# A gated mix of a state-space layer and linear attention on one core: the written-out step list is replaced by another order of the same steps

## The chip, the cores and the metric

The kernel runs on one core of one Trainium2 chip. The metric is the device time of one execution in microseconds (us), taken without the profiler; three runs of the kernel before gave 156.17, 156.59 and 157.39 us, median 156.59. One further execution was profiled, and every number about single instructions comes from it.

The engines are named as in the profile: PE (TensorE, matrix products; PEld are its weight loads), ACT (ScalarE, functions and evictions of PSUM), DVE (VectorE), POOL (GpSimd) and SP (SyncE, which issues most of the DMAs). Each runs its own list of instructions in order and waits for the others by semaphores.

## The reference, cut to what matters

```python
x = A_x                                    # (1, 2048, 512), bf16
g = sigmoid((x * gate_w).sum(-1))          # one gate for each row
# A: a diagonal complex recurrence, 512 states
h[t] = Lam_bar * h[t-1] + x[t] @ B_bar.T   # Lam_bar = exp(dt * Lam), dt = exp(log_dt)
a = 2 * (h @ C.T).real + x * Dskip
# B: linear attention, 32 heads of 16
q, k, v = split(x @ wqkv)
pq, pk = q @ w_phi, k @ w_phi              # per head, 16 x 16
phi = concat(softmax(p), softmax(-p))      # for p = pq and p = pk: 32 features
kv, z = phi_k.T @ v, phi_k.sum(rows)
b = (phi_q @ kv) / (phi_q @ z + 1e-6) @ wo
out = g * a + (1 - g) * b
```

## The kernel before, in words

The 2048 rows are 16 tiles of 128. Row t is put in the tile of its residue t mod 8, so that the recurrence becomes eight interleaved sequences of 256 steps (two tiles each); x is held transposed (xT). The weights w_phi are folded into the query and key weights (steps W, f, w), so a tile's features come from one product.

The program is written as some 190 small generators, called steps, each of which issues a few instructions and yields. A string ORDER names the steps one by one; a loop goes through it and calls `next` on the step that each word names. So ORDER is the order in which the instructions of PE, ACT, DVE and SP are recorded, and with a manual schedule it is the order in which each of these engines runs them. A word is a step's name, then possibly `@` with the PSUM banks for its outputs, then possibly `:D` (this eviction on DVE instead of ACT) or `:A` (this output store issued from ACT's queue instead of SP's). `F:28` puts 28 dummy products on PE.

The steps that matter here (the lines are those of the kernel before):

- W0 to W3: PE transposes a block of the key weights, an eviction copies it to SBUF (line 121 on ACT, 123 on DVE). f0 to f3: the fold of w_phi into the key weights, with one eviction each. V: a PE transpose and DVE copy of the state parameters, from which U, P, P2, P3, P4 and i0 to i3 make decay rates and the tables of sines and cosines. The sines are ACT's function Sin.
- k0 to k15, v0 to v15, q0 to q15: key features, values and query features of a tile, four or eight matmuls and their evictions.
- x, n, e, s: the two softmaxes of a group of tiles. x and n (DVE, lines 519 to 535) are a tree of maxima and one of minima and the differences. e (ACT, line 140) is one Exp of 128x1024 a tile. s is a tree of sums (DVE), then Ln (ACT), Exp of its negative (ACT) and a product (DVE, line 556). The key groups 0 to 4 hold 2, 2, 4, 4 and 4 tiles. The query groups are A, 1, 2 and 3 (X1, N1, E1, S1 and so on); their s ends with an Exp called rho, a product (line 567) and DMA transposes into phT (line 579), one a tile; two tiles of group 3 are transposed on PE.
- a0 to a4: PE adds up phi_k.T @ v. Y: DVE takes it from PSUM.
- g (r, j): 8 matmuls and more for B_bar x of residue r and state block j, evicted into uv (ACT); z (j): the scan over 256 steps on DVE; h (r, j): the states of the other residues. c0 to c7: the scaled C weights, two products on ACT (line 603) and a sum on DVE; J, C, Q, R, l, NI, NR, O: input loads and DMA transposes, all issued by SP.
- y0 to y15: PE, a = h C + x Dskip of one tile, in a PSUM bank that stays open. o0 to o15: PE forms numerator and denominator (pn, line 753), ACT takes Ln and Exp for the division and the gate, DVE multiplies, and the result is transposed, by DMA (line 775) or for o12 to o15 on PE. t0 to t15: PE adds o @ wo to the open bank (line 782), an eviction scales by the gate (line 786 on ACT, 788 on DVE), a DMA stores the tile (line 790).
- L: closes the pool of the tables' temporaries, opens the one of the scan, and calls `pin_act_set` (line 131). ACT evaluates functions from a loaded set. `pin_act_set` records a load of the set `natural_log_exp_and_others`, which holds both Exp and Ln. Where a function is not in the set that was loaded last, the build puts a load ahead of it by itself.

```python
    def pin_act_set():
        pre = nc.scalar.preload_act_table_set(ACT_SET)
...
    def st_L():
        pin_act_set()
        tab_g.__exit__(None, None, None)
        enter("sw", name="ssm", bufs=2)
        yield
```

`pin_act_set` is called twice: once ahead of the list (line 171), and once in L. The Sin of the tables needs a set of its own, so that before the first e there is no longer a set with Exp loaded.

Of the kernel before, what the change touches and what calls it, by code (L numbers as in the profile page):

```python
# [23 lines left out]
ORDER = """
NI l8 l10 F:28 W1@0 W0@1 W0 B W2@2 W2 NR W1:D W3@3 f1@4 f1 W3:D V@5 V U f0@6 U P P P2 U P2 P2 P2 P2 f0 f2@0 P4 P4 P4
V2@1 V2 f2 l9 P3 i3 f3@3 f3 F:4 k1@2 k0@4 P P2 P3 l12 i1 i0 k0 gw i0 i3 U k1 i3 i3:D i3 i0 i1 i1 k2@5 k2 k3@6 k3 v0@03
k4@1 i0:D x0 i1:D l11 x0 i1 n0 F:4 x0 k4 n0 R0 i2 n0 i0 x0 n0 k5@4 i2 i2 x0 i2:D n0 x1 x1 k5 n1 i2 v3@25 v0 x1 k7@6 k7
k6@7 R1 L e0 n1 n1 x1 n1 l13 k6:D v4@14 x1 l14 v1@03 v1 k10@6 n1 x2 v4 n2 n2 n2 x2 e0 s0 x2 v3 v7@70 v7 l15 k8@3 v2@14
v6@25 s0 s0 k9@7 k12@0 x2 Q1 e1 s0 v2 v6 s0 k11@1 s0 e1 M k11 k8 D k10 k9 R3 k12 g40@4 g40 s0 s1 g00@2 g00 n2 a0@51 a0
v5@36 v5 s1 R5 x2 v8@70 R2 v8 C5 s1 s1 s1 s1 g60@4 n2 x3 s1 g60 g30@2 x3 n3 x3 n3 g10@3 C3 g20@6 e2 e2 e2 e2 x3 a1 a1  # L30
n3 Q2 k15@7 g10 g10 k15 x3 n3 g20 k14@0 k14 s2 n3 R4 s2 k13@4 g01@3 Q0 k13 n4 s2 g30 g01 x4 s2 x4 Q3 n4 x4 g50@7 g70@6
g30 g50 n4 x4 e3 e3 g41@0 g50 n4 R7 s2 g21@4 s2 g70 s2 C7 e3 g31@3 e3 s3 g62@2 C4 g70 g70 z0 g11@7 a2 z0 s3 g41 z0 a2
a2 s3 C6 g21 g62 C2 C1 g11 g11 C0 J0 w0@6 w1@0 J2 J2 a2 g22@4 J0 w2@2 x4 s3 J1 g31 w1 w0 w3@7 g22 g31 z0 z0 z0 s3 w2
s3 n4 z0 z0 w3 g61@0 g51@6 g51 g61 g02@4 g51 e4 g02 g71@3 g71 g71 g71 q3@2 s3 g12@7 g12 e4 q2@0 z0 g12 z1 q3 q1@6 q1
q0@4 q2 z1 z0 h50@3 z1 z1 g42@7 q0 z1 z1 v10@26 h50 xA z1 h10@0 e4 e4 z1 g42 nA s4 g32@4 v10 g32 a3 g52@3 g32 h60@7 c2
xA s4 c4 O g52 xA c4 R6 z1 z1 v9@26 s4 h10 g52 nA g72@4 g72 c4 h60 v9 a3 J3 g03@3 v11@26 c2 c2 s4 g72 g72 c0 c0 nA
g63@0 z2 z2 v12@74 a3 nA v11 a3 xA g03 z2 z2 z2 z2 xA nA s4 J3 g63 g23@2 c5 s4 v12 g23 h51@6 g13@3 g13 g13 z2 z2 c0 z2
z2 eA g43@0 g43 eA v14@74 v14 J1 h51 s4 g33@2 g33 h52@3 g33 h12@0 g53@6 eA g53 g53 h12 h11@7 h11 h52 eA sA g73@4 g73
g73 g73 v13@26 v13 q10@0 z3 c6 z3 c5 sA z3 z3 v15@73 z3 a4 a4 a4 v15 z3 q10 q5@4 a4 Y z3 h31@0 q5 sA h30@4 z3 q9@2 h31
q13@6 h31 q9 h33@0 h61@7 Y q13 h30 sA sA c5 h62@3 z3 z3 h30 h61 sA Y Y h22@5 q4@2 h62 q4 h33 q15@6 q11@7 h22 h20@4 h20  # L40
h32@2 h32 sA sA c1 q11 h13@1 h13 h32 q14@3 h40@5 h33 c3 h53@7 h42@4 sA h42 h53 c1 c1 sA h21@2 c3 h21 q6@0 q6 q15 c6
q7@1 h63@4 h63 q8@7 h03@0 c3 q7 c6 h40 sA c7 h41@6 h41 y6@2 c7 h03 h03 h43@4 h43 y2@1 h02@5 c7 sA h23@6 h23 h01@0
h00@4 END q8 G X1 y6 y6 q14 y2 N1 X1 h00 h00 N1 y2 h02 h02 X1 N1 G h01 o0@6 y0@7 o0 o0@3 h01 o2@4 o2 X1 o2@5 o2 o2 N1
y5@6 o0 y3@0 X1 N1 y5 X2 o0 o1@4 E1 o2 y0 o2 o0 E1 E1 E1 X2 y1@5 y1 y3 y3 o1 G N2 X2 N2 X2 o0 N2 X2 o3@3 o3 o3@4 S1 o3
o3 G S1 N2 S1 t2 o3 S1 o3 t2 t2:A q12@3 q12 N2 S1 S1 o1@4 o1 o1 o1 o1 S1 S1 E2 S1 y0 y4@1 y9@3 y8@4 y8 y8 X3 E2 E2 S1
S1 S1 N3 X3 E2 t3 X3 X3 X3 S2 N3 t0 t0 t0:A S2 t3 S2 y1 t1 t1 y5 y9 y9 o4@7 o4 o4@0 o4 y4 o4 o4 o4 o5@5 o5 o5@7 o5 o5
y13@0 S2 S2 o6@5 o6 o6@7 o6 o6 y13 N3 y7@5 y7 N3 y7 y13 o5 S2 S2 N3 E3 o5 o6 o6 S2 S2 E3 E3 o7@7 o7:D y4 t4 t4:D t5
o7@7 S2 S2 E3 S3 t5 S2 S3 S3 o7 o7 o7 t6 y11@1 y11 o7 t6 o8@6 o8 o8@7 o8 o8 S3 S3 o8 y12@2 o9@6 o9 o9@7 o8 y11 y12 y12
y10@6 o9 o9 o9 o11@7 o11 o9 S3 S3 y10 y10 o11@7 t7 o11 o11 t7 t8 S3 S3 o11 o11 S3 t8 S3@7 S3:D S3@5 S3 t9 t9 t1:A
o10@4 y15@7 o10:D o10@5 o10:D t8 o10 o10 o10 y15 o12@4 o12:D o12@3 t4 o14@5 o12 o12 o12 t5 o14 t11 o14@4 o14:D o14 o14  # L50
t11 y14@3 t9:A o13@5 o13 o12@4 o12:D y14 o13@1 o13 o13 o15@4 o15:D o15@5 o15 o15 t12 t3:A t10 o13 o13@1 o15 t6:A t11
o14@4 o13:D t7 t10 t10 y15 t12 t12 o15@5 o15 y14 o14:D t13 t14 t14 t14 t13 t13 t15 t15 t15:A
"""
# [811 lines left out]
```

## Time and profile before

| | |
|---|---|
| time, median of three runs | 156.59 us (156.17 to 157.39) |
| profiled execution: span from the first to the last instruction (its time as a whole is not listed) | 153.7 us |
| PE busy | 145.5 us (95%) |
| DVE busy | 131.0 us (85%) |
| ACT busy | 136.7 us (89%) |
| mean granted TensorE clock | 0.995 |
| bytes by DMA | 17.03 MB |

The profile's page lists the busy time of each engine and the chain of work that ended last. Further views group instructions by line, give the busy time of each engine in chosen windows of the span, and list instructions in order of time: start, length, engine, line, operation, the tiles written and read, and, in square brackets, how long the engine sat idle before it and what ended that. A row with x4 merges four instructions that follow each other. A matmul's row is longer than the distance to the next one, since PE pipelines them, and ACT's rows overlap a little for the same reason, so the distance between starts is the better measure of what an instruction costs.

### The profile page before, as it was taken

Reading aid. Unit: us, or ns where it says so; the run is one execution under the profiler, and the core shown is the slowest. Engines: PE = TensorE matmul, PEld = TensorE weight load, DVE = VectorE, ACT = ScalarE, POOL = GpSimd, SP = SyncE. Lnnn points to the kernel's source line nnn. Section 1 sums busy time; section 2 is a strip of 40 time slices with the busy share of each in tenths; the row PEclk is TensorE's granted clock in tenths of the full one; section 3 lists DMA queues with packets and bytes.
Section 4 is the critical chain, followed back from the end, with each engine's and each line's share of the span. In section 5 each row is a group of like instructions: output and inputs, shape, how many; then the busy total and the mean of one; then the engine's idle time right before and its main releaser. Section 6 shows DMA issues by size and latency. Waiting matters only on the chain.

```text
span 153.7 us, 3412 instructions
## 1 busy us (share of the span) xinstructions
PE 145.5 (95%) x1238; PEld 99.7 (65%) x1254; DVE 131.0 (85%) x302; ACT 136.7 (89%) x322; POOL 12.9 (8%) x43
## 2 busy tenths in 40 slices
...
GB/s 117 162 220 121 213 171 102 102 86 92 101 102 100 80 146 205 237 133 0 2 4 2 0 0 134 125 18 68 33 82 118 215 80 194 141 118 172 211 123 102
DMA packets 48737, 17.03 MB, mean 111 GB/s; under 512 B 42064, under 2 KB 48720, under 8 KB 48720
## 3 DMA queue, kind: packets, MB, share of 16 engines
...
q8 instruction: 10, 0.16, 0.5%
q0 software_dynamic: 160, 0.01, 0.2%
q14 instruction: 7, 0.06, 0.1%
...
## 4 chain that ended last, share of the span: by engine, by line
ACT 48%; PE 31%; DMA 8%; DVE 6%; issue 3%; POOL 2%; ACTq 0%; POOLq 0%
PE py L734 12%; ACT EEk L140 12%; ACT uv L121 9%; PE py L782 6%; ACT vx L121 5%; PE pq L478 5%; ACT Xq L121 5%; ACT phT L603 4%; PE ph L685 3%; ACT va L121 3%; DMA phT<-EEq 3%; DMA oT<-on 3%; PE pn L753 2%; DMA vec_n<-in_A_log_dt_dram 2%; ACT EEq L140 2%
## 5 line engine op out<-in xcount | busy, mean ns | idle before, releaser
L614 PE MATMUL pgq<-xT,BT 128*128 128x256 bf16 x256 | 31.5, 272 | 0.0
L614 PEld LDWEIGHTS <-BT 128*128 128x128 bf16 x256 | 24.7, 98 | 3.5
L140 ACT ACTIVATE EEk<-EEk 128x1024 bf16<-128x1024 bf16 x20 | 21.3, 1099 | 0.0
L478 PEld LDWEIGHTS <-xT 128*128 128x128 bf16 x128 | 12.2, 97 | 11.0 <-issue 0.2
L121 ACT CAST uv<-pgq 128x512 bf16<-128x512 f32 x28 | 16.7, 638 | 0.0
L492 PE MATMUL pv<-Wv,xT 128*128 128x256 bf16 (+1 forms) x128 | 16.5, 273 | 0.1
L478 PE MATMUL pq<-Wq,xT 128*128 128x512 bf16 x60 | 15.2, 379 | 0.2
L782 PE MATMUL py<-Wo,oT 128*128 128x512 bf16 x59 | 14.7, 379 | 0.6 <-DMA oT<-on 0.3
L478 PE MATMUL pk<-Wk,xT 128*128 128x512 bf16 x60 | 14.9, 379 | 0.2
L492 PEld LDWEIGHTS <-xT 128*128 128x128 bf16 x128 | 12.5, 98 | 3.1 <-issue 0.2
L786 ACT ACTIVATE ot<-py,G 128x512 bf16<-128x512 f32 x15 | 9.8, 684 | 2.9 <-PE py L782 2.4
L140 ACT ACTIVATE EEq<-EEq 128x1024 bf16<-128x1024 bf16 x12 | 11.8, 1084 | 0.3 <-DVE EEq L535 0.3
L603 ACT ACTIVATE phT<-X,dgB 128x512 bf16<-128x512 bf16 x16 | 11.1, 751 | 0.0
L140 ACT ACTIVATE ld<-pn 128x16 f32<-128x16 f32 x32 | 6.4, 204 | 5.2 <-PE pn L753 5.0
L121 ACT CAST vx<-pv 128x256 bf16<-128x256 f32 x32 | 10.7, 435 | 0.0
L121 ACT CAST nu<-pn 128x256 bf16<-128x256 f32 x26 | 10.0, 400 | 0.0
L556 DVE TENSOR_TENSOR EEk<-EEk,rck 128x4096 bf16<-128x4096 bf16 (+1 forms) x5 | 9.3, 1860 | 0.1
L121 ACT CAST Xq<-pq 128x512 bf16<-128x512 f32 x16 | 9.0, 604 | 0.4 <-PE pn L753 0.4
L782 PEld LDWEIGHTS <-oT 128*128 128x128 bf16 x64 | 5.7, 98 | 5.7 <-DMA oT<-on 0.5
L753 PEld LDWEIGHTS <-phT 128*128 128x128 bf16 x128 | 6.4, 97 | 4.6 <-DMA phT<-EEq 1.3
L761 DVE TENSOR_TENSOR on<-nu,rd 128x512 bf16<-128x512 bf16 x16 | 6.6, 422 | 2.6 <-ACT rd L140 2.1
L519 DVE TENSOR_TENSOR smk<-smk 128x512 bf16<-128x512 bf16 (+4 forms) x18 | 8.1, 449 | 0.1
...
## 6 DMA issues: line engine op xcount, KB each, us to landing
...
out_dram<-ot SPq DMA_DIRECT2D x9, 128.0 KB, 2.2
out_dram<-ot ACTq DMA_DIRECT2D x7, 128.0 KB, 2.0
...
```

What stands on the lines that cost most here:

```text
L121: nc.scalar.copy(out=out_ap, in_=in_ap)
L140: ins = nc.scalar.activation(**kw)
L478: MM(out=pt[:], lhsT=xT[:, kt, ti * P:(ti + 1) * P], rhs=W[:, kt, :], start=(kt == 0), stop=(kt == KT - 1))
L492: MM(out=pv[c][:], lhsT=xT[:, kt, ti * P:(ti + 1) * P], rhs=Wvg[:, kt, c * hd:(c + 1) * hd + c], start=(kt == 0), stop=(kt == KT - 1))
L519: VT(out=dst, in0=cur[:, :, :, 0:n, :], in1=cur[:, :, :, n:2 * n, :], op=op)
L556: VT(out=E5, in0=E5, in1=rc.to_broadcast([P, L, 2 * NB, Dh, 4]), op=ALU.mult)
L603: nc.scalar.mul(out=t_, in_=x_, mul=c_)
L614: MM(out=pg[:, h, :], lhsT=BT[:, kt, 2 * j + h, :], rhs=xT[:, kt, r * NC:(r + 1) * NC], start=(h == 0 and kt == 0), stop=(r % 2 == 0 and k ...
L734: MM(out=py[:], lhsT=hs(r, t, slice(a * P, (a + 1) * P)), rhs=C2B[t], start=(t == 0), stop=False)
L753: MM(out=pn[:, 4 * m:4 * m + 4, :].rearrange("p h e -> p (h e)"), lhsT=ph[:, 4 * hf + m, :], rhs=KVm[:, 4 * hf + m, :], start=(m == 0), st ...
L782: MM(out=py[:], lhsT=oT[:, g, :], rhs=Wo[:, g, :], start=False, stop=(g == HG - 1))
L786: nc.scalar.mul(out=ot[:], in_=py[:], mul=G[:, ti:ti + 1])
```

## The change

The string ORDER is replaced by another one, with the same 862 words apart from banks and sides; no generator changes. The new string has one line more, so that each line number after it is one higher. The core of the diff:

```diff
-NI l8 l10 F:28 W1@0 W0@1 W0 B W2@2 W2 NR W1:D W3@3 f1@4 f1 W3:D V@5 V U f0@6 U P P P2 U P2 P2 P2 P2 f0 f2@0 P4 P4 P4
-V2@1 V2 f2 l9 P3 i3 f3@3 f3 F:4 k1@2 k0@4 P P2 P3 l12 i1 i0 k0 gw i0 i3 U k1 i3 i3:D i3 i0 i1 i1 k2@5 k2 k3@6 k3 v0@03
-k4@1 i0:D x0 i1:D l11 x0 i1 n0 F:4 x0 k4 n0 R0 i2 n0 i0 x0 n0 k5@4 i2 i2 x0 i2:D n0 x1 x1 k5 n1 i2 v3@25 v0 x1 k7@6 k7
-k6@7 R1 L e0 n1 n1 x1 n1 l13 k6:D v4@14 x1 l14 v1@03 v1 k10@6 n1 x2 v4 n2 n2 n2 x2 e0 s0 x2 v3 v7@70 v7 l15 k8@3 v2@14
-v6@25 s0 s0 k9@7 k12@0 x2 Q1 e1 s0 v2 v6 s0 k11@1 s0 e1 M k11 k8 D k10 k9 R3 k12 g40@4 g40 s0 s1 g00@2 g00 n2 a0@51 a0
-v5@36 v5 s1 R5 x2 v8@70 R2 v8 C5 s1 s1 s1 s1 g60@4 n2 x3 s1 g60 g30@2 x3 n3 x3 n3 g10@3 C3 g20@6 e2 e2 e2 e2 x3 a1 a1
-n3 Q2 k15@7 g10 g10 k15 x3 n3 g20 k14@0 k14 s2 n3 R4 s2 k13@4 g01@3 Q0 k13 n4 s2 g30 g01 x4 s2 x4 Q3 n4 x4 g50@7 g70@6
-g30 g50 n4 x4 e3 e3 g41@0 g50 n4 R7 s2 g21@4 s2 g70 s2 C7 e3 g31@3 e3 s3 g62@2 C4 g70 g70 z0 g11@7 a2 z0 s3 g41 z0 a2
...
-y5@6 o0 y3@0 X1 N1 y5 X2 o0 o1@4 E1 o2 y0 o2 o0 E1 E1 E1 X2 y1@5 y1 y3 y3 o1 G N2 X2 N2 X2 o0 N2 X2 o3@3 o3 o3@4 S1 o3
-o3 G S1 N2 S1 t2 o3 S1 o3 t2 t2:A q12@3 q12 N2 S1 S1 o1@4 o1 o1 o1 o1 S1 S1 E2 S1 y0 y4@1 y9@3 y8@4 y8 y8 X3 E2 E2 S1
-S1 S1 N3 X3 E2 t3 X3 X3 X3 S2 N3 t0 t0 t0:A S2 t3 S2 y1 t1 t1 y5 y9 y9 o4@7 o4 o4@0 o4 y4 o4 o4 o4 o5@5 o5 o5@7 o5 o5
-y13@0 S2 S2 o6@5 o6 o6@7 o6 o6 y13 N3 y7@5 y7 N3 y7 y13 o5 S2 S2 N3 E3 o5 o6 o6 S2 S2 E3 E3 o7@7 o7:D y4 t4 t4:D t5
-o7@7 S2 S2 E3 S3 t5 S2 S3 S3 o7 o7 o7 t6 y11@1 y11 o7 t6 o8@6 o8 o8@7 o8 o8 S3 S3 o8 y12@2 o9@6 o9 o9@7 o8 y11 y12 y12
-y10@6 o9 o9 o9 o11@7 o11 o9 S3 S3 y10 y10 o11@7 t7 o11 o11 t7 t8 S3 S3 o11 o11 S3 t8 S3@7 S3:D S3@5 S3 t9 t9 t1:A
-o10@4 y15@7 o10:D o10@5 o10:D t8 o10 o10 o10 y15 o12@4 o12:D o12@3 t4 o14@5 o12 o12 o12 t5 o14 t11 o14@4 o14:D o14 o14
-t11 y14@3 t9:A o13@5 o13 o12@4 o12:D y14 o13@1 o13 o13 o15@4 o15:D o15@5 o15 o15 t12 t3:A t10 o13 o13@1 o15 t6:A t11
-o14@4 o13:D t7 t10 t10 y15 t12 t12 o15@5 o15 y14 o14:D t13 t14 t14 t14 t13 t13 t15 t15 t15:A
+F:28 W0@3 W0 W1@4 B W2@1 W3@6 l10 l8 NI W1:D f1@2 NR W2:D W3:D f1:D l9 f2@4 V@6 V l11 f2 U l12 P P f0@5 f0 l14 R0 R1
+P2 l15 P2 P2 P2 f3@0 U P2 V2@4 V2 P4 f3 P F:4 P2 k1@6 k1 k0@3 k0 gw P4 P4 P3 P3 l13 i3 i1 Q1 i0 k3@1 U i0 i3 i1 k2@0
+i3 i0 v0@46 i3:D i3 i1 i1:D R4 R2 n0 k2 v0 k4@5 C3 k3 i0:D R3 n0 x0 F:4 i1 k5@3 n0 i2 R5 x0 i0 C2 v1@10 n0 k4 x0 i2 x0
+i2 k5 v4@47 i2:D k6@2 k7@3 i2 x0 x1 n0 e0 n1 x1 n1 n1 k7 x1 v1 C4 n1 k6:D x1 Q3 k10@6 U e0 x1 n1 n2 v3@52 v4 x2 n2 s0
+s0 v3 v7@31 v7 x2 k8@0 k8 s0 x2 s0 v2@47 v2 v6@35 C1 M D k9@2 s0 k11@0 k12@1 e1 s0 s0 e1 s1 g40@4 v6 k12 k11 k9 g40 C5
+k10 g00@3 a0@51 g00 a0 v5@07 v5 n2 s1 n2 v8@42 s1 x2 g60@6 Q0 s1 s1 v8 x2 k14@7 x3 s1 g20@0 g60 n2 s1 e2 e2 e2 e2
+k13@3 a1 a1 Q2 g10@2 g10 g20 g10 k15@4 R6 k15 n3 g30@6 k13 x3 n3 x3 n3 x3 g01@0 n3 x3 k14 s2 n3 s2 g30 g01 x4 g21@4
+g30 e3 g50@0 g31@7 s2 e3 x4 s2 s2 n4 n4 x4 L g50 g50 s2 n4 g62@2 g70@6 x4 n4 e3 e3 g70 g70 g70 g41@0 s2 g41 g21 s3
+g11@3 g11 g11 C7 a2 a2 a2 a2 z0 z0 s3 z0 z0 C6 z0 w0@6 s3 w1@0 O w1 z0 s3 g62 z0 g22@4 g22 w2@3 w2 z0 g31 x4 g31 g61@2
+g61 s3 w0 g51@4 g51 s3 g51 g02@7 g02 w3@6 g71@2 g71 n4 s3 w3 q0@4 q1@7 e4 q3@6 g71 g71 e4 q0 z0 z1 z1 q3 q2@2 q2 z0 z1
+q1 C0 J0 J2 J1 J2 g12@0 g12 h10@3 J1 g12 h50@2 z1 z1 z1 e4 h10 nA g42@4 g72@7 g32@0 g42 xA h50 z1 z1 c2 xA e4 g32
...
+h03 q8 y6 h00@0 y2 h02@6 q14 h01@3 h23 h43 END X1 N1 h00 h00 y2 y0@7 G X1 h02 o0@5 o0 o0@4 N1 X1 o0 N1 h02 y0 o2@0 o2
+o2@4 X1 o2 h01 h01 y1@5 y5@6 N1 o2 o0 o3@4 X1 N1 X2 o2 o0 X2 G o1@3 X2 y3@0 y1 y1 N2 X2 o2 N2 y3 X2 E1 E1 E1 E1 S1 N2
+o1 o3 y0 y5 t2 o3@3 o3 S1 o3 t2 o3 o0 t0 y5 t0 o1@3 o1 S1 q12@4 q12 y3 N2 y4@1 S1 S1 y8@3 y8 y8 N2 S1 y6 o1 o1 o3 o1
+S1 t3 S1 S1 S1 y4 y9@4 S1 S1 t1 E2 E2 E2 X3 X3 y4 t3 E2 t1 o4@7 o4 o4@0 N3 X3 o4 N3 o4 y9 y9 X3 o5@7 o5 o5@5 o5 o5 N3
+y13@0 o6@7 X3 S2 S2 o6 o4 S2 N3 o6@5 o6 S2 S2 o5 y13 N3 y13 o7@7 o6 y7@5 y7 S2 o7 S2 o4 t4 E3 E3 E3 o5 o6 o6 S2 t5
+t4:D o7@7 S2 S2 E3 o7:D y11@1 t6 y11 t5 t6 y7 o7 S2 o8@7 o8 S3 S3 o7 S3 o8@6 y12@2 o8 o8 o9@7 o8 o9 o9@6 y12 y12 o9 S3
+y10@6 y10 y10 o9 S2 o7 o8 o11@7 o9 y11 t7 S3 S3 t5:A o9 S3 o11 S3 S3 t7:D o11@7 t1:A o11 o11 o11 t8 t8:D S3 S3@7 S3
+S3@5 S3:D t9 t8:A o11 t9:D o10@3 o10:D o10@5 o10 y15@7 o14@5 t4:A t7 o12@4 o10 o12:D o12@3 o12 o14 y15 y15 o14@4 o13@5
+o12 o10 o13:D o13@3 o14:D t11 o14 o15@5 t0 o13:D y14@4 o12 o15:D o12@3 o13 o14 o15@5 o15 o10 t3 y14 y14 o13 o15 o15
+t10 o12 t9 t11 t11:A o14@3 o15@5 o15 o13@1 o13 o14:D t12 t10:D t12:D t14 t15 t10 t14:D t13 t2 t13:D t15 t12:A t14:A
+t13:A t6 t15
```

What moves, by the order of the built instructions:

- L goes from the fourth line of the list, ahead of e0, to the eighth, behind e0, e1, e2, the first two words of e3, and the Ln of s0, s1 and s2. The built list of ACT holds 3 loads of function sets before, 9 after.
- The evictions of W2 and f1 go from ACT to DVE. In the last quarter of the list the scalings of t7, t8, t9, t10, t12, t13 and t14 go from ACT to DVE, and some small evictions of o7, o10, o12, o13 and S3 change sides both ways. SP issues eight of the 16 output stores, ACT eight; before, nine and seven. The stores of t0, t2 and t6 come much later in the list.
- Up to the last word of E1, ACT's list holds the same instructions in both, apart from the six loads and the evictions of W2 and f1. PE's products ahead of o4 are nearly the same ones in both.
- The order of g, h, q, v, c and y among each other changes nearly everywhere, and with it the order of the loads and DMA transposes on SP.

18 lines of the change are left out of this document (7 added, 11 removed).

## The prediction

> **What bounds the kernel now.** I read the page's busy times first, then the view by windows, then the timeline of ACT, then the chain that ended last.
>
> ```profile
> span 153.7 us, 3412 instructions
> ...
> PE 145.5 (95%) x1238; PEld 99.7 (65%) x1254; DVE 131.0 (85%) x302; ACT 136.7 (89%) x322; POOL 12.9 (8%) x43
> ...
> ACT 48%; PE 31%; DMA 8%; DVE 6%; issue 3%; POOL 2%; ACTq 0%; POOLq 0%
> ```
>
> Three engines are nearly full and the chain runs through two of them, so no one engine "is" the bound over the whole span. The windows (length, then busy microseconds of PE, PEld, DVE, ACT, POOL) say where each of them is full:
>
> ```profile
> 0.00:10.00 10.00, 7.81 (x73) 6.42 (x75) 5.66 (x37) 5.64 (x10) 4.92 (x17) 1.00 0.62 162
> ...
> 18.00:46.00 28.00, 27.87 (x256) 21.74 (x256) 27.69 (x54) 27.86 (x63) 0.66 (x3) 1.00 0.64 114
> 46.00:100.00 54.00, 53.42 (x479) 40.31 (x480) 53.38 (x113) 53.65 (x116) 0.00 (x0) 1.00 0.41 84
> 100.00:107.30 7.30, 7.24 (x52) 3.73 (x52) 7.30 (x18) 7.30 (x20) 0.00 (x0) 1.00 0.19 42
> 107.30:118.10 10.80, 10.69 (x77) 5.75 (x77) 10.56 (x20) 9.38 (x22) 0.00 (x0) 1.00 0.55 74
> 118.10:149.60 31.50, 30.54 (x268) 17.03 (x270) 18.48 (x39) 23.82 (x75) 0.00 (x0) 1.00 0.66 156
> ```
>
> From 18 to 107.3 us ACT is idle for 0.14 + 0.35 + 0.00 = 0.5 us in 89. After that it has room: 1.4 us up to 118.1 and 7.7 us up to 149.6. PE is full to the end: from 118.1 to 149.6 it is idle for 0.96 us only. So anything put on ACT before 107.3 us has no hole to fall into, and anything that delays PE at 118 us moves the end.
>
> Busy time can flatter an engine whose rows overlap, so I look at the pitch of ACT's rows. Each row is start, length, engine, line:
>
> ```profile
> 8.86 0.21 ACT L140 ACTIVATE ssm_par<-ssm_par 128x4 f32<-128x4 f32 x1
> 9.09 1.28 ACT L146 ACT_TABLE_LOAD   x1
> ...
> 16.93 0.64 ACT L121 CAST Xq<-pk 128x512 bf16<-128x512 f32 x1
> 17.59 1.28 ACT L132 ACT_TABLE_LOAD   x1
> 18.89 1.06 ACT L140 ACTIVATE EEk<-EEk 128x1024 bf16<-128x1024 bf16 x1
> ...
> 32.51 3.90 ACT L140 ACTIVATE EEk<-EEk 128x1024 bf16<-128x1024 bf16 x4
> 36.31 0.57 ACT L121 CAST uv<-pgq 128x512 bf16<-128x512 f32 x1
> 36.78 0.59 ACT L121 CAST Xq<-pk 128x512 bf16<-128x512 f32 x1
> ```
>
> Four exponentials start 0.95 us apart (32.51 to 36.31), a 512-wide eviction is followed after 0.47 us (36.31 to 36.78): ACT issues without a gap. And a table load is not free: the eviction of 16.93 would be followed at 17.40, but the load waits for its end (17.57), starts at 17.59, takes 1.28, and the exponential starts at 18.89. The load costs 18.89 - 17.40 = 1.49 us of ACT there; its bare length is 1.28.
>
> **The change part by part.** The order listing of the two built programs shows the same 1254 matmuls and the same arithmetic. Four things differ.
>
> *1. Table loads.* In the old list the step L (the load of the set that has both Exp and Ln) stands before the first exponential, e0. In the new list it stands far behind, after group 2's Ln; e0, e1, e2 and the sums s0, s1, s2 run before it. Then the build puts a load wherever the next function isn't in the loaded set. The built ACT lists have 3 loads before and 9 after: one before e0, then before the Ln and again before the next Exp of s0/e1, the same two for s1, one for the Ln of s2, and L itself. That is six more, all between e0 (18.89 us in the old run) and the last exponentials of e3, in the chain
>
> ```profile
> 42.94 1.89 ACT EEk L140 x2
> ```
>
> where ACT has 0.14 us to spare. Bare price 6 x 1.28 = 7.7; with the drain of the row above, 6 x 1.49 = 8.9. The Trainium skill (ScalarE: Activation LUTs, "What ACT_TABLE_LOAD costs") gives 1283 ns for a load plus about 1380 ns of drain, 2.66 us for a switch. The trace agrees on the load and not on the drain: the exponential starts 0.02 us after the load. By the page the term would be 6 x 2.66 = 16 us (an estimate).
>
> *2. Two evictions leave ACT early.* W2 and f1 go to DVE.
>
> ```profile
> 5.39 1.07 ACT L121 COPY Xq<-ptw 128x512 bf16<-128x512 bf16 x2 [2.22 <-PE ptw L277]
> ...
> 4.12 0.69 DVE L346 TENSOR_TENSOR BD<-Wc,mask 128x512 bf16<-128x512 bf16 x1 [1.42 <-DMA Wc<-in_B_w_phi_dram]
> 4.97 0.42 DVE L123 COPY Xq<-ptw 128x512 bf16<-128x512 bf16 x1 [0.16 <-PE ptw L277]
> 5.97 0.42 DVE L123 COPY Xq<-ptw 128x512 bf16<-128x512 bf16 x1 [0.57 <-PE ptw L277]
> 6.98 0.17 DVE L315 CAST vec<-pvt 128x12 f32<-128x12 bf16 x1 [0.59 <-PE pvt L313]
> ```
>
> They take 1.0 off ACT (the row of two copies is 1.07 long with its tail, so some 0.5 each, and 0.47 is the pitch of a 512-wide cast above). On DVE they cost 0.42 for the copy and about 0.6 for the cast (nearest row: a 512-wide f32 vector operation, below, 0.68), 1.0 in all, ahead of the step V. DVE idles 0.16 + 0.57 + 0.59 = 1.3 us there, which hides them; uncovered, they'd delay the table chain by 1.0.
>
> Everything else that ACT does up to the last exponential of E1 (the first query group) is the same set of instructions in both lists, only permuted. So ACT's stock of work at that point grows by 7.7 to 8.9 less 1.0: **6.7 to 7.9 us**. I take 7.2, nearer the bare load, because its waits on others (at most the 0.5 us above) vanish when it is the late one.
>
> *3. What E1 releases.* The timelines of ACT, DVE, SP and PE around it, then the median landing from the page's DMA issues, then one row of the chain:
>
> ```profile
> 103.50 4.00 ACT L140 ACTIVATE EEq<-EEq 128x1024 bf16<-128x1024 bf16 x4
> ...
> 107.54 1.23 DVE L519 TENSOR_TENSOR smq<-EEq 128x2048 bf16<-128x2048 bf16 x1
> ...
> 112.41 1.22 DVE L567 TENSOR_TENSOR EEq<-EEq,rhoq 128x2048 bf16<-128x2048 bf16 x1
> ...
> 113.80 6.68 SPq L579 DMA_TRANSPOSE phT<-EEq  x4
> ...
> 118.18 0.42 PE L753 MATMUL pn<-KVm,phT 128*128 128x68 bf16 x8
> ...
> 119.83 0.43 PE L753 MATMUL pn<-KVm,phT 128*128 128x68 bf16 x8 [0.36 <-DMA phT<-EEq]
> ...
> phT<-EEq SPq DMA_TRANSPOSE x10, 2.8
> ...
> 115.15 4.63 DMA phT<-EEq
> ```
>
> E1 ends at 107.5, the sum tree starts at 107.54, the product with rho ends at 113.63, the transposes are issued from 113.80. The first lands about 2.8 us later, 116.6, and o4's matmuls (118.18) come 1.6 us after it. The second, issued at 115.15, lands at 119.78, and o5 starts at 119.83: no slack. So a delay of 7.2 at E1 reaches PE as 5.6 (o4) to 7.2 (o5). The second transpose shared the DMA engines with the store of t0, which the new list moves away from there, so I count 1.0 of slack: 6.2. In both lists the same PE work lies behind o4, the 30.5 busy us of the last window, and its 0.96 us of holes are all that can be given back; I take half, 0.5.
>
> *4. The end, and the DMA queues.* Seven scalings of the output tile (line 786), those of t7 to t10 and t12 to t14, go from ACT to DVE; of the steps o and S3 a few small evictions change sides both ways.
>
> ```profile
> L786 ACT ACTIVATE ot<-py,G 128x512 bf16<-128x512 f32 x15 | 9.8, 684 | 2.9 <-PE py L782 2.4 <-ACT ot L786 0.4
> ...
> L689 DVE TENSOR_TENSOR HM<-ph,uv 128x512 bf16<-128x512 f32 x8 | 5.3, 682 | 0.0
> ...
> 110.09 0.36 ACTq L790 DMA_DIRECT2D out_dram<-ot  x1
> ...
> 148.80 1.84 ACT L786 ACTIVATE ot<-py,G 128x512 bf16<-128x512 f32 x3 [1.10 <-PE py L782]
> ...
> out_dram<-ot SPq DMA_DIRECT2D x9, 128.0 KB, 2.2
> ```
>
> The last three scalings stand in line on ACT (1.84 us). Split over two engines the last one ends about one place, 0.6 us, sooner (a DVE form of that width isn't in the trace; the nearest row is 0.68, the same as ACT's 0.684). Against it, two early stores (t2, t6) are held back to the end of SP's list: two more issues, at about 0.35 us each, and 256 KB more in the last 3 us. Below: nothing, since t15's store waits for its scaling anyway; above 0.7. I take 0.2. Net of the end: -0.4. The input loads, transposes and J copies are permuted on SP early; with ACT late they have more time, so nothing, and 1.35 us (the first two issues above are 1.35 apart) for one that were out of place. One store more on ACT's queue lies in ACT's idle 7.7 us.
>
> Sum: 7.2 - 1.0 - 0.5 - 0.4 = +5.3 us. The profile gives its execution's span alone: 153.7 becomes 159.0. The median of the runs, 156.6, is 2.9 above it, and that stays. **156.6 + 5.3 = 161.9 us.**
>
> **The rivals.**
> *The loads are hidden.* PE, not ACT, sets the pace, and each load falls into a wait of ACT. For it: the chain runs through PE lines for 31%, and PE is as full as ACT. Against: ACT's 0.5 us of idle in 89. Time: the ends of the list alone, about 156.6 - 0.4 = 156.2.
> *Faster.* PE at its own pace, with its holes closed by the new order: 0.13 + 0.58 + 0.06 + 0.11 + 0.96 = 1.8 us from 18 us on, and 0.4 at the end. It needs ACT to reach the end of E1 no later than 107.5 + 1.0; then 154.4. PE's 2.2 idle us of the first 10 stay: ACT's first eviction (5.39) still waits for the transposes of the same weights.
> *It adds up.* All six at 1.49, the 1.0 us on DVE uncovered, no slack at o5, nothing given back: 8.9 - 1.0 + 1.0 = +8.9, 165.5. For it: all engines run their lists in order, so a late ACT can make PE and DVE late for each other too. Against: whoever waits for a late ACT gains time on everything else that it would have waited for.
> *The full drain.* If after each load ACT stood still for about its own length again, the shift would be near 6 x 2.6 = 15.6, less 1.0, 1.0, 0.5 and 0.4: 169.3. Row 18.89 speaks against it. The Trainium skill's section on table loads named above is what would have it so.
> That the loads aren't there is no case: the built list has them, and the three that the old built list has are the three in its trace.
>
> **How the numbers follow.** Forecast 0.72 (159 to 164.5), adding up 0.13, full drain 0.03, hidden 0.07, faster 0.05. One per cent, 1.6 us, is about what a measurement of this kernel tells from no change (its runs lie within 156.17 to 157.39). Slower 0.72 + 0.13 + 0.03 = 0.88, within 1% 0.07, faster 0.05. The range takes in the forecast and the adding-up case with its price at either end: low 6.7 - 1.6 - 1.0 - 0.6 = +3.5 would be 160, and I go to 157.8 for half-hidden loads; high 166.5.
>
> **What would show it.** Right: nine table loads in the groups of the profile after, those on line 141 with 1.28 us each between 19 and 50 us; ACT full and PE with holes of 4 to 6 us in that stretch; the last E1 exponential ending near 114.7 instead of 107.5; o4 on PE near 124; from there to the last matmul 31 us again. Wrong: ACT waiting just before its loads (hidden), E1 ending before 109 (faster), or E1 late and the last matmul not (then the tail had slack that I don't see).

## The result and the profile after

The new list takes **165.16 us** (median of four runs, 165.10 to 165.41) against 156.50 us (156.17 to 157.39) for the old one: a ratio of **1.056, interval 1.052 to 1.059**, so 8.7 us more. The prediction was 161.9 us, with 157.8 to 166.5 as its range. The time lies in the range, but 3.3 us above the forecast and outside the forecast's own band of 159 to 164.5; it is within 0.4 us of the rival "it adds up" (165.5). Of the experiments below, one execution of new_l_early_oldsp (160.47 us) and one of new_to_E1_old_tail (159.89) were over 1.5% longer than the fastest of their kernel and are left out of the medians.

The page of the kernel after, its span, busy times, clock in 40 slices and the shares of the chain that ended last:

```profile
span 163.4 us, 3418 instructions
...
PE 148.4 (91%) x1238; PEld 100.1 (61%) x1254; DVE 136.3 (83%) x310; ACT 140.8 (86%) x320; POOL 14.7 (9%) x43
...
PEclk9999999997899999999999999999999999999998
...
PE 57%; ACT 26%; DMA 8%; DVE 6%; issue 1%
```

The span grew by 9.7 us. Busy time grew by 4.1 on ACT, 2.9 on PE and 5.3 on DVE, so each of the three idles more than before: a wait was added, not just work. The profiled execution of before was a short one: the timed runs, before and after, last 2.0 us longer than their spans (165.41 and 163.4), so its time was some 155.7 us (an estimate: 153.7 + 2.0), 0.8 below the median, where the prediction took 2.9 from a single profile. That is why 9.7 us of span are 8.7 us of time. All shifts against rows of before, below, are shifts against that short execution; where in it the 0.8 us were saved no run shows.

The view by windows of the kernel after (length, then busy us of PE, PEld, DVE, ACT, POOL; then clock, DMA share and GB/s):

```profile
18.00:46.00 28.00, 23.66 (x183) 16.28 (x184) 23.11 (x47) 27.28 (x58) 3.88 (x8) 0.94 0.70 128
46.00:100.00 54.00, 52.07 (x492) 41.09 (x493) 49.76 (x106) 53.62 (x112) 0.00 (x0) 1.00 0.35 65
...
128.00:159.50 31.50, 28.81 (x247) 16.29 (x252) 20.79 (x41) 20.62 (x65) 0.00 (x0) 1.00 0.69 152
```

From 18 to 46 us ACT is nearly as full as it was (0.72 us idle against 0.14), and PE and DVE, which had been full too, idle 4.3 and 4.9 us. That is the place of the loss. In the last 31.5 us before the last product PE idles 2.7 us, where it idled 0.96 before: a second, smaller loss.

The timeline of ACT in the first stretch (start, length, engine, line, then what ended the idle time):

```profile
16.94 1.28 ACT L141 ACT_TABLE_LOAD   x1
18.24 1.06 ACT L141 ACTIVATE EEk<-EEk 128x1024 bf16<-128x1024 bf16 x1
19.20 0.57 ACT L122 CAST Xq<-pk 128x512 bf16<-128x512 f32 x1
...
24.29 1.28 ACT L141 ACT_TABLE_LOAD   x1
25.58 0.31 ACT L141 ACTIVATE lgk<-smk 128x128 f32<-128x128 f32 x1
25.91 1.28 ACT L141 ACT_TABLE_LOAD   x1
27.20 1.06 ACT L141 ACTIVATE EEk<-EEk 128x1024 bf16<-128x1024 bf16 x1
...
43.00 1.56 ACT L122 CAST Xq<-pk 128x512 bf16<-128x512 f32 x3 [0.41 <-PE pk L479]
44.74 1.07 ACT L122 CAST uv<-pgq 128x512 bf16<-128x512 f32 x2 [0.18 <-PE pgq L615]
...
47.74 1.28 ACT L141 ACT_TABLE_LOAD   x1
49.03 0.42 ACT L141 ACTIVATE lgk<-smk 128x256 f32<-128x256 f32 x1
49.47 1.28 ACT L133 ACT_TABLE_LOAD   x1
50.76 0.58 ACT L122 CAST uv<-pgq 128x512 bf16<-128x512 f32 x1
...
51.56 1.99 ACT L141 ACTIVATE EEk<-EEk 128x1024 bf16<-128x1024 bf16 x2
```

The same two exponentials of e3 in the kernel before:

```profile
42.85 1.99 ACT L140 ACTIVATE EEk<-EEk 128x1024 bf16<-128x1024 bf16 x2
```

The loads stand where the prediction put them: one round each Ln, with the next row 0.01 to 0.02 us behind each. The last exponentials of e3 start 51.56 - 42.85 = 8.71 us later. That sum can be taken apart: e0 starts 0.65 us earlier (18.24 against 18.89), six loads are 7.70, two waits for PE are 0.41 + 0.18 = 0.59, and ACT has one key eviction more between e0 and e3 (nine casts from pk into Xq, as the one at 19.20, against eight; before, it stood ahead of e0), which is 0.47 us at the pitch of such casts. 8.71 + 0.65 - 7.70 - 0.59 - 0.47 = 0.60 us is left for six loads, 0.10 each, beside the 1.28.

The groups of ACT's loads (times, busy us, mean ns):

```profile
L141 ACT ACT_TABLE_LOAD x6 | 7.7, 1283 | 0.1
...
L133 ACT ACT_TABLE_LOAD x2 | 2.6, 1283 | 1.9 <-issue 1.9
...
L147 ACT ACT_TABLE_LOAD x1 | 1.3, 1283 | 0.0
```

Nine, as forecast. From e3 on the shift hardly changes. The timelines of ACT, SP and PE round E1 in the kernel after:

```profile
112.29 3.94 ACT L141 ACTIVATE EEq<-EEq 128x1024 bf16<-128x1024 bf16 x4
...
122.75 6.53 SPq L580 DMA_TRANSPOSE phT<-EEq  x4
...
126.48 0.42 PE L754 MATMUL pn<-KVm,phT 128*128 128x68 bf16 x8
...
128.73 0.43 PE L754 MATMUL pn<-KVm,phT 128*128 128x68 bf16 x8 [0.75 <-DMA phT<-EEq]
```

Against the rows of before: E1 +8.79, the transposes of S1 +8.95, o4 +8.30, o5 +8.90. The end, from PE's timeline, the chain and DVE's timeline:

```profile
139.23 5.07 DMA oT<-on
...
144.35 1.04 PE L783 MATMUL py<-Wo,oT 128*128 128x512 bf16 x4 [1.69 <-DMA oT<-on]
...
155.97 3.62 PE L783 MATMUL py<-Wo,oT 128*128 128x512 bf16 x15
...
159.63 0.75 DVE L789 TENSOR_SCALAR ot<-py,G 128x512 bf16<-128x512 f32 x1 [0.97 <-PE py L783]
```

The last product ends at 159.59 instead of 149.62: +9.97, that is o4's 8.30 and 1.7 us of new holes. One hole of 1.69 us stands ahead of t7, which waits for the DMA transposes of o7.

### The profile page after: what moved, and what is told of

Read it like the earlier page. It is cut to its first block, busy times and chain, and to the rows that moved or that the text cites. A ratio compares the mean times of both kernels' runs of the same rounds, so it can differ in the third digit from the quotient of the medians.

```text
span 163.4 us, 3418 instructions
## 1 busy us (share of the span) xinstructions
PE 148.4 (91%) x1238; PEld 100.1 (61%) x1254; DVE 136.3 (83%) x310; ACT 140.8 (86%) x320; POOL 14.7 (9%) x43
## 4 chain that ended last, share of the span: by engine, by line
PE 57%; ACT 26%; DMA 8%; DVE 6%; issue 1%
PE pgq L615 12%; PE py L735 12%; PE pq L479 8%; PE py L783 7%; ACT L141 5%; ACT EEk L141 5%; PE ph L686 4%; PE pv L493 4%; DMA oT<-on 3%; ACT vx L122 3%; ACT Xq L122 3%; DMA phT<-EEq 3%; ACT uv L122 2%; PE pn L754 2%; DMA C2r<-in_B_wqkv_dram 2%; PE kvacc L595 2%
## 5 line engine op out<-in xcount | busy, mean ns | idle before, releaser
L615 PE MATMUL pgq<-xT,BT 128*128 128x256 bf16 x256 | 32.7, 277 | 2.2 <-ACT vx L122 1.9
L479 PEld LDWEIGHTS <-xT 128*128 128x128 bf16 x128 | 12.3, 99 | 11.6 <-issue 0.5
L604 ACT ACTIVATE phT<-X,dgB 128x512 bf16<-128x512 bf16 x16 | 11.9, 765 | 0.0
L789 DVE TENSOR_SCALAR ot<-py,G 128x512 bf16<-128x512 f32 x8 | 6.0, 749 | 4.9 <-PE py L783 4.8
L122 ACT CAST nu<-pn 128x256 bf16<-128x256 f32 x25 | 9.2, 387 | 0.0
L122 ACT CAST Xq<-pk 128x512 bf16<-128x512 f32 x15 | 8.5, 608 | 0.4 <-PE pk L479 0.4
```

The lines of the kernel that those rows point to most:

```text
L122: nc.scalar.copy(out=out_ap, in_=in_ap)
L479: MM(out=pt[:], lhsT=xT[:, kt, ti * P:(ti + 1) * P], rhs=W[:, kt, :], start=(kt == 0), stop=(kt == KT - 1))
L604: nc.scalar.mul(out=t_, in_=x_, mul=c_)
L615: MM(out=pg[:, h, :], lhsT=BT[:, kt, 2 * j + h, :], rhs=xT[:, kt, r * NC:(r + 1) * NC], start=(h == 0 and kt == 0), stop=(r % 2 == 0 and k ...
```

## The experiments

The theory was that six loads on a full ACT make the loss, whatever else the new order does. The rivals were that the new order itself makes it (through PE, SP's transfers or the end), and that a single one of the other edits does. All comparisons are with the kernel before on the same chip. Each of these kernels computes the whole output; where the words Z add loads, they load the set that is loaded already, so they change nothing but time.

### The new order without the loads: new_l_early

```diff
-i2 k5 v4@47 i2:D k6@2 k7@3 i2 x0 x1 n0 e0 n1 x1 n1 n1 k7 x1 v1 C4 n1 k6:D x1 Q3 k10@6 U e0 x1 n1 n2 v3@52 v4 x2 n2 s0
+i2 k5 v4@47 i2:D k6@2 k7@3 i2 x0 x1 n0 L e0 n1 x1 n1 n1 k7 x1 v1 C4 n1 k6:D x1 Q3 k10@6 U e0 x1 n1 n2 v3@52 v4 x2 n2 s0
...
-g30 e3 g50@0 g31@7 s2 e3 x4 s2 s2 n4 n4 x4 L g50 g50 s2 n4 g62@2 g70@6 x4 n4 e3 e3 g70 g70 g70 g41@0 s2 g41 g21 s3
+g30 e3 g50@0 g31@7 s2 e3 x4 s2 s2 n4 n4 x4 g50 g50 s2 n4 g62@2 g70@6 x4 n4 e3 e3 g70 g70 g70 g41@0 s2 g41 g21 s3
```

> The new list with the word L moved back to just ahead of e0: 3 table loads instead of 9, all else as in the new list. Theory A (the six loads on a full ACT are the whole loss, and the permutation is worth about nothing): 165.2 - 8.8 = 156.4 us, between 155.5 and 157.0, and the last exponential of E1 starts near 106.3 as in the old list. Theory B (the new order itself is worse, the loads cost only what they can't hide): 160 to 163 us, E1 near 110.

Measured: 160.09 against 156.85 us, ratio 1.021 (1.018 to 1.024): +3.2 us. With three loads the new list is 5 us faster than with nine, but the permutation has a price of its own. That is the time of theory B; theory A, by which the permutation is worth nothing, fails here, and so does the prediction, which had it as a gain (-1.0 for the two evictions, -0.4 for the end). Its waits (who waits for whom: us in total, times, longest) show where a part of it is:

```profile
PEld L435 <- DMA HM<-in_B_wqkv_dram: 1.4, 2, 0.8
ACT phT L604 <- DMA X<-HM: 1.4, 1, 1.4
```

The first is for a transposed weight block (a step Q), the second for a copy J; both were moved on SP's list. In the kernel after, with its nine loads, neither wait is there.

### The loads without the new order: old_l_late

```diff
-k6@7 R1 L e0 n1 n1 x1 n1 l13 k6:D v4@14 x1 l14 v1@03 v1 k10@6 n1 x2 v4 n2 n2 n2 x2 e0 s0 x2 v3 v7@70 v7 l15 k8@3 v2@14
+k6@7 R1 e0 n1 n1 x1 n1 l13 k6:D v4@14 x1 l14 v1@03 v1 k10@6 n1 x2 v4 n2 n2 n2 x2 e0 s0 x2 v3 v7@70 v7 l15 k8@3 v2@14
...
-g30 g50 n4 x4 e3 e3 g41@0 g50 n4 R7 s2 g21@4 s2 g70 s2 C7 e3 g31@3 e3 s3 g62@2 C4 g70 g70 z0 g11@7 a2 z0 s3 g41 z0 a2
+g30 g50 n4 x4 e3 e3 g41@0 g50 n4 R7 s2 L g21@4 s2 g70 s2 C7 e3 g31@3 e3 s3 g62@2 C4 g70 g70 z0 g11@7 a2 z0 s3 g41 z0 a2
```

> The old list with L moved behind the Ln of s2, where the new list has it: 9 loads instead of 3, nothing else moved. Theory A: six loads of 1.28 plus the drain of about 0.19 each, 8.9 us on ACT; no eviction moved and at most 1 us of slack behind E1, so 156.5 + 8 to 9 = 164.5 to 165.5 us. Theory B: 158 to 160 us, since in the old order they would be partly hidden.

Measured: 165.20 against 156.85 us, ratio 1.052 (1.050 to 1.055): +8.35 us, as theory A had it. One word moved in the old list costs as much as the whole change. Its ACT timeline, the windows, and PE's first products of o4:

```profile
19.10 1.06 ACT L140 ACTIVATE EEk<-EEk 128x1024 bf16<-128x1024 bf16 x1
...
52.02 1.99 ACT L140 ACTIVATE EEk<-EEk 128x1024 bf16<-128x1024 bf16 x2
...
18.00:46.00 28.00, 23.28 (x184) 16.30 (x184) 22.71 (x45) 27.35 (x56) 0.79 (x4) 0.94 0.61 114
46.00:100.00 54.00, 51.43 (x493) 41.22 (x494) 49.56 (x105) 53.56 (x112) 0.00 (x0) 1.00 0.36 67
...
127.35 0.42 PE L753 MATMUL pn<-KVm,phT 128*128 128x68 bf16 x8
```

From e0 to e3 the list takes 52.02 - 19.10 = 32.92 us where it took 23.96: +8.96, or 1.49 a load. Of that, 0.52 us are two new waits of ACT for PE (0.23 and 0.29, between 42 and 46 us); without them it is 8.44, or 1.41 a load. At e3 the shift is 9.17, and at o4 it is 9.17 still (127.35 against 118.18). In the rows nothing is given back in 75 us. The windows have the pattern of the kernel after: PE 4.7 us idle in the first stretch.

### Is it ACT's time, or the place of L? old_z6_mid

L stays where it was; a new word Z loads the same set again, six times between 24 and 47 us.

```diff
-v6@25 s0 s0 k9@7 k12@0 x2 Q1 e1 s0 v2 v6 s0 k11@1 s0 e1 M k11 k8 D k10 k9 R3 k12 g40@4 g40 s0 s1 g00@2 g00 n2 a0@51 a0
+v6@25 s0 s0 k9@7 k12@0 x2 Q1 e1 s0 v2 Z:1 v6 s0 k11@1 s0 e1 M k11 k8 D k10 k9 Z:1 R3 k12 g40@4 g40 s0 s1 g00@2 g00 n2 a0@51 a0
...
+        if tok == "Z":
+            for _ in range(int(eng)):
+                act_st["pre"] = nc.scalar.preload_act_table_set(ACT_SET)
+            continue
```

> The old list with L in its place and six superfluous loads of the same set put behind the steps v2, k9, v5, v8, g1 0 and k13, which run between 24 and 37 us. Theory A: as old_l_late, 164.5 to 165.5 us, since only ACT's time counts. Theory C (what hurts is that L, which also changes the pools, comes late): near 156.5 us.

Measured: 164.62 against 156.85 us, ratio 1.048 (1.046 to 1.051): +7.8 us, 1.30 a load. So the loss needs neither L's late place nor loads beside the Ln: six loads at other places of the full stretch make 7.8 of the 8.35 us.

### Half the loads: old_l_mid

```diff
-v5@36 v5 s1 R5 x2 v8@70 R2 v8 C5 s1 s1 s1 s1 g60@4 n2 x3 s1 g60 g30@2 x3 n3 x3 n3 g10@3 C3 g20@6 e2 e2 e2 e2 x3 a1 a1
+v5@36 v5 s1 R5 x2 v8@70 R2 v8 C5 s1 s1 L s1 s1 g60@4 n2 x3 s1 g60 g30@2 x3 n3 x3 n3 g10@3 C3 g20@6 e2 e2 e2 e2 x3 a1 a1
```

(and L taken out ahead of e0, as above; three loads more instead of six)

> The old list with L just ahead of the Ln of s1: 6 loads instead of 3. If each load costs its length and the drain, 1.49 us, and nothing of it is hidden: 156.85 + 4.5 = 161.3 us, half of what six cost. If the first ones are hidden and only a pile of them hurts: 157 to 159 us.

Measured: 160.23 against 156.73 us, ratio 1.023 (1.020 to 1.025): +3.5 us, 1.17 a load, somewhat less than the load's own 1.28 and 1.1 us below the expected 161.3. The price is about in proportion to the count, 1.2 to 1.4 a load by the times. The first and the last exponential of e0 to e3, from ACT's timeline:

```profile
19.13 1.06 ACT L140 ACTIVATE EEk<-EEk 128x1024 bf16<-128x1024 bf16 x1
...
47.22 1.99 ACT L140 ACTIVATE EEk<-EEk 128x1024 bf16<-128x1024 bf16 x2
```

From e0 to e3 that is 28.09 us against 23.96, +4.13, or 1.38 a load, with no wait of ACT for PE in the stretch.

### The loads where ACT idles: old_z6_tail

The six words Z stand behind the last E3 and behind the scalings of t6, t7, t8, t9 and t11, in the stretch where the prediction counted 7.7 us of idle ACT.

```diff
-o7@7 S2 S2 E3 S3 t5 S2 S3 S3 o7 o7 o7 t6 y11@1 y11 o7 t6 o8@6 o8 o8@7 o8 o8 S3 S3 o8 y12@2 o9@6 o9 o9@7 o8 y11 y12 y12
+o7@7 S2 S2 E3 Z:1 S3 t5 S2 S3 S3 o7 o7 o7 t6 y11@1 y11 o7 t6 Z:1 o8@6 o8 o8@7 o8 o8 S3 S3 o8 y12@2 o9@6 o9 o9@7 o8 y11 y12 y12
...
```

> The old list with six superfluous loads of the same set late: behind the last word of E3 and behind the scalings of t6, t7, t8, t9 and t11, from about 127 to 142 us, where ACT is idle for a quarter of the time. Theory A: ACT has 7.7 us to spare there, but a load can stand ahead of a Ln that PE's next products wait for; 156.5 to 159 us. Theory D (a load costs its length wherever it stands): 164 to 165.5 us.

Measured: 162.25 against 156.85 us, ratio 1.034 (1.029 to 1.038): +5.4 us, 0.9 a load, between the two expectations. The waits of this kernel:

```profile
DVE nu L123 <- ACT ld L140: 8.5, 4, 4.6
```

In the kernel before that wait is 4.5 us in all. The small Ln and Exp of the steps o stand between two products of PE, and a load ahead of them delays the next one. ACT's idle time there is made of such short waits; in the kernel before none of its waits for pn was longer than 1.2 us, so there was no room for 1.3 us at once:

```profile
ACT ld L140 <- PE pn L753: 5.0, 8, 1.2
```

### Two evictions on DVE: old_w2f1_d

```diff
-NI l8 l10 F:28 W1@0 W0@1 W0 B W2@2 W2 NR W1:D W3@3 f1@4 f1 W3:D V@5 V U f0@6 U P P P2 U P2 P2 P2 P2 f0 f2@0 P4 P4 P4
+NI l8 l10 F:28 W1@0 W0@1 W0 B W2@2 W2:D NR W1:D W3@3 f1@4 f1:D W3:D V@5 V U f0@6 U P P P2 U P2 P2 P2 P2 f0 f2@0 P4 P4 P4
```

> The old list with the evictions of W2 and f1 on DVE, as in the new list. By the prediction ACT, full up to E1, is 1.0 us earlier: 155.9 us. Rival: ACT waits for PE's folds and DVE's chain of small steps starts later, so nothing is gained: 156.6 to 157.5 us.

Measured: 157.03 against 156.73 us, ratio 1.001 (0.999 to 1.003): no gain. The ACT timeline of this kernel:

```profile
8.26 0.20 ACT L140 ACTIVATE ssm_par<-vec 128x4 f32<-128x4 f32 x1 [2.71 <-DVE vec L315]
```

That row stood at 7.19 before, behind a wait of 0.23. ACT has 1.0 us less to do, and spends more than that waiting for V on DVE, behind the two evictions that it was rid of: e0 starts at 19.92 us where it started at 18.89. (The profiled execution, 157.52 us, was the longest of the twelve.)

### Seven scalings on DVE: old_t_sides

```diff
-y10@6 o9 o9 o9 o11@7 o11 o9 S3 S3 y10 y10 o11@7 t7 o11 o11 t7 t8 S3 S3 o11 o11 S3 t8 S3@7 S3:D S3@5 S3 t9 t9 t1:A
+y10@6 o9 o9 o9 o11@7 o11 o9 S3 S3 y10 y10 o11@7 t7 o11 o11 t7:D t8 S3 S3 o11 o11 S3 t8:D S3@7 S3:D S3@5 S3 t9 t9:D t1:A
...
-o14@4 o13:D t7 t10 t10 y15 t12 t12 o15@5 o15 y14 o14:D t13 t14 t14 t14 t13 t13 t15 t15 t15:A
+o14@4 o13:D t7 t10:D t10 y15 t12:D t12 o15@5 o15 y14 o14:D t13 t14 t14:D t14 t13:D t13 t15 t15 t15:A
```

> The old list with the scalings of t7 to t10 and t12 to t14 on DVE, as in the new list; the stores stay where they are. By the prediction the last scalings no longer stand in line on ACT: -0.4 to -0.6 us, 156.3 us. Rival: DVE has the products of o ahead of them there, and the end doesn't move or comes later: 156.85 to 157.5 us.

Measured: 158.75 against 156.73 us, ratio 1.012 (1.008 to 1.017): +2.0 us, more than either expectation. DVE's timeline says why:

```profile
137.51 0.75 DVE L788 TENSOR_SCALAR ot<-py,G 128x512 bf16<-128x512 f32 x1 [3.34 <-PE py L782]
138.18 1.22 DVE L567 TENSOR_TENSOR EEq<-EEq,rhoq 128x2048 bf16<-128x2048 bf16 x1
```

DVE waits 3.34 us for t7's product, and the product of S3 with rho, which stood at 133.89, is queued behind it. In the new list t7's scaling comes after S3's product, so this run shows a trap of the old order, and does not price the scalings in the new one.

### SP's order by itself: new_l_early_oldsp and new_oldsp

In both, the words l, N, R, Q, C, J and O of the new list stand in the old list's sequence; the first has L early, the second L late as in the change.

```diff
-F:28 W0@3 W0 W1@4 B W2@1 W3@6 l10 l8 NI W1:D f1@2 NR W2:D W3:D f1:D l9 f2@4 V@6 V l11 f2 U l12 P P f0@5 f0 l14 R0 R1
+F:28 W0@3 W0 W1@4 B W2@1 W3@6 NI l8 l10 W1:D f1@2 NR W2:D W3:D f1:D l9 f2@4 V@6 V l12 f2 U l11 P P f0@5 f0 R0 R1 l13
...
```

> The new list with L ahead of e0, and at the places of SP's words (l, N, R, Q, C, J, O) the same words in the sequence of the old list; all compute words as in the new list. Theory E (without the table loads to cover them, the later arrival of Q2 and of the J copies costs the 3.2 us that the new list with L early lost against the old one): 156.5 to 157.5 us, and the waits of PE for HM and of ACT for X go. Theory F (the order of the compute words costs it): 159 to 160.5 us.

> The new list as it is, L late and nine table loads, but SP's words in the sequence of the old list. Theory H (with the loads on ACT the later input transposes are waited for by nobody, so their order costs nothing): 164.6 to 165.5 us. If both losses add: 163.2 us.

Measured: with L early 157.84 against 156.73 us, ratio 1.008 (1.005 to 1.011), so SP's order makes about 2 of the 3.2 us (3.24 - 1.11), and the two waits for transfers shown above are gone. With L late 165.58 against 156.77, ratio 1.058 (1.054 to 1.062): the same as the change itself. The windows 46 to 100 us of new_l_early and new_l_early_oldsp, one fence each:

```profile
46.00:100.00 54.00, 51.46 (x470) 39.13 (x473) 50.44 (x106) 51.07 (x112) 0.00 (x0) 1.00 0.36 73
```

```profile
46.00:100.00 54.00, 53.99 (x494) 41.08 (x493) 53.08 (x110) 53.64 (x118) 0.00 (x0) 1.00 0.39 80
```

With SP's new order ACT idles 2.9 us there and PE 2.5; with the old one 0.4 and nothing. Late transfers cost about 2 us when ACT is on time, and nothing that the times show when six loads make it late.

### Head and end by themselves: old_to_E1_new_tail and new_to_E1_old_tail

The first is the old list up to the last word of E1 and then what is left in the new sequence, with the new sides and banks. The second is the new list up to there, with L early and SP's old order, and then what is left in the old sequence.

```diff
-y5@6 o0 y3@0 X1 N1 y5 X2 o0 o1@4 E1 o2 y0 o2 o0 E1 E1 E1 X2 y1@5 y1 y3 y3 o1 G N2 X2 N2 X2 o0 N2 X2 o3@3 o3 o3@4 S1 o3
+o2@5 o2 o2 N1 y5@6 o0 y3@0 X1 N1 y5 X2 o0 o1@4 E1 o2 y0 o2 o0 E1 E1 E1 G y1@5 o3@4 X2 G X2 y1
...
```

> The old list up to the last word of E1, then all words that are left in the sequence of the new list, with the new list's banks and sides. It holds the new end alone, with L early and SP's loads as of old. By the prediction (the end gains 0.4, some holes of PE are closed): 155.8 to 156.5 us. Theory G (the new end has waits of its own, as between o12 and the last product of the new list with L early and the old loads): 157.7 to 158.4 us.

> The new list up to the last word of E1, with L ahead of e0 and SP's words in the old sequence, then all words that are left in the sequence of the old list. Theory G: the 1.4 us that this list lost with its own end go, 156.5 to 157.2 us. If the loss stood before E1: 158 us.

Measured: old head with new end 159.18 against 156.77 us, ratio 1.016 (1.012 to 1.020), +2.4. New head with old end 157.59 against 156.77, ratio 1.005 (1.002 to 1.008), +0.8. The new end is a loss, not a gain of 0.4; but 2.4 us, more than either expectation, is not its price, as the rows show. A window, PE's timeline and a wait of old_to_E1_new_tail:

```profile
108.80 0.29 PE L756 MATMUL pn<-KVm,phT 128*128 128x68 bf16 x4 [1.63 <-ACT nu L124]
...
128.00:138.00 10.00, 8.70 (x72) 4.75 (x72) 6.27 (x11) 6.70 (x20) 0.00 (x0) 1.00 0.78 172
...
138.05 1.04 PE L785 MATMUL py<-Wo,oT 128*128 128x512 bf16 x4 [1.35 <-DMA oT<-on]
...
DVE ot L791 <- DMA out_dram<-ot: 1.0, 1, 1.0
```

PE's busy time in that window was 9.55 us before. The hole of 1.35 us is the one of the kernel after, ahead of t7, behind o7's transposes; and one scaling waits 1.0 us for a store, because the tile whose buffer it needs is stored late now. The hole of 1.63 us at 108.80 stands where the old head meets the new sequence, and neither the kernel before nor the kernel after has it. A comparison without that seam is the time from o4's first product to the end of the last product, in which PE has the same work in each list (268 weight loads): with the old end 31.44 us (before), 31.75 (old_l_late) and 31.75 (new_to_E1_old_tail); with the new end 33.11 (after), 32.53 (new_l_early), 33.11 (new_l_early_oldsp), 32.57 (new_oldsp) and 32.45 (here). On average the new end is 1.1 us longer. By the times the new end on the new head costs 157.84 - 157.59 = 0.25 us more than the old one, which is within the noise of the two. No list that was tried is faster than the kernel before.

## Why the prediction was right, and which terms were wrong

The direction and the cause were right: nine loads, the six new ones in the stretch named, PE's holes of 4 to 6 us beside them (4.3 from 18 to 46 us), and old_l_late shows that the loads suffice for the whole loss. The size was not: the range held because it reached up to the price of the rival "it adds up", while the forecast of +5.3 us fell short, because its term for the loads was small and no term taken off from it came true.

**Step 1, the loads.** The mechanism was right and the term too small. The prediction took 7.2 us for the net delay of ACT, near the bare load, because ACT's waits on others would "vanish when it is the late one". Measured: +8.96 us from e0 to e3 for old_l_late, +8.35 in its time. ACT's waits did not vanish; 0.5 to 0.6 us were added between 42 and 46 us (see the last section). The upper price of step 1, 6 x 1.49 = 8.9, came out by some luck: a load by itself cost 1.38 to 1.41 us in the rows (old_l_mid, old_l_late), and the waits for PE, which the step did not have, made up the rest.

**Step 2, W2 and f1 on DVE.** The term -1.0 failed. Alone the edit is worth nothing (1.001); in the trace after, e0 came 0.65 us earlier, but 0.47 of that is the key eviction which now stands behind e0. The "uncovered" case of the step came true in old_w2f1_d: the chain of V started 1.07 us later.

**Step 3, slack behind E1.** The terms -1.0 and -0.5 failed. The last exponential of E1 ended at 116.2 us (112.29 + 3.94) where the prediction said 114.7, o4 came at 126.5 instead of 124, and from there to the end of the last product it took 33.1 us, not 31. The step asked only how late E1 may be, as if PE had no lateness of its own. But PE needs ACT's evictions and DVE's products from e0 on: in old_l_late o4 is as late as e3, 9.17 us. Behind the last load (from 55 us to the end of E1) all three engines were full again: in old_l_late PE 60.5, DVE 60.7 and ACT 60.9 of 61.3 us. So nothing could be caught up, and the slack of 1.6 us at o4 was no slack, since the work ahead of it was as late as its operand. The 1.0 us of slack at o5 had another reason, the store of t0 beside the second transpose. In the kernel after that store is gone from there, and the chain has for the transpose

```profile
124.11 4.58 DMA phT<-EEq
```

which is the 4.63 us of before: the store had not held it up. The holes behind o4 did not shrink by 0.5 but grew from 0.96 to 2.7 us. The objection to "it adds up", that a waiting engine gains time on everything else, did not hold here, where the late engine had no hole of its own to catch up in.

**Step 4, the end.** The term -0.4 failed in sign. At the very end it is there: from the last product's end to the last scaling's end it took 1.02 us (150.64 - 149.62) and takes 0.79 (160.38 - 159.59). But ahead of it the new order makes the way from o4 to the last product 0.7 to 1.7 us longer in the five lists that have it, in the kernel after through PE waiting 1.69 us for o7's transposes; the step had looked at scalings and stores, and not at the transposes that the products ahead of them wait for.

**SP's order at nothing "with ACT late".** Right, and now with a price: new_oldsp is no faster than the change, and without the loads the same order costs about 2 us.

**The rivals.** "It adds up" hit the time nearly (165.5), with the right reasons for the two evictions and the slack; it was partly luck, since it had the loads at 1.49 us, where they cost 1.38 to 1.41 by themselves, and no term for the end. "Hidden" and "faster" fell with old_l_late and new_l_early: even without its loads the new order is slower. "Full drain", 169.3, would have needed about 2.6 us a load; the row behind each load starts within 0.02 us of its end. The Trainium skill (ScalarE: Activation LUTs, "What ACT_TABLE_LOAD costs") has 1283 ns for the load and about 1380 ns of drain. The groups show the load to the digit; of a drain they and the rows show 0.1 us (old_l_mid: 1.38 us a load).

**What the parts add up to.** +8.35 (loads alone) and +3.2 (order alone) are 11.6 us; together they cost 8.7. About 2 us of the difference is SP's order, which the loads cover. The rest is under 1 us. In the rows the kernel after reaches o4 0.87 us ahead of old_l_late (126.48 against 127.35), as it had started e0 0.86 us ahead (18.24 against 19.10), and then loses 1.36 us to it in the end (33.11 against 31.75).
